# Where the first batch's zeros, masks and plain values are made: VectorE and GpSimd against ScalarE and SyncE

## Chip, cores and metric

One of the eight cores of a Trainium2 chip runs the kernel. The metric is the device time of one execution in microseconds (us); lower is better. A core has five engines with queues of their own: TensorE (PE; its weight loads are listed as PEld), VectorE (DVE), ScalarE (ACT), GpSimd (POOL) and SyncE (SP). The last two issue most of the DMAs here.

## The reference

Attention with a local mask, followed by a feed-forward network (FFN) with a squared ReLU:

```python
# q, k, v: (8 batches, 8 heads, 576 positions, 64), float32
scores = q @ k.T / 8
rel = pos[:, None] - pos[None, :]
mask_plain = (rel >= 0) & (rel < 32)                      # heads 0 to 3
mask_dil = (rel >= 0) & (rel < 128) & (rel % 4 == 0)      # heads 4 to 7
attn = softmax(where(mask, scores, -1e9))
x = (attn @ v) as (4608 tokens, 512)
h = maximum(x @ w_in, 0)          # w_in: (512, 2048)
out = (h * h) @ w_out             # w_out: (2048, 512)
```

## The kernel before

Everything is computed in bf16 with f32 accumulation. Heads are taken in pairs e = 0 to 3; pairs 0 and 1 are the plain ones, 2 and 3 the dilated ones. A batch's 576 positions fall into nine blocks of 64. A pair's values lie block-diagonally in a tile `vbd[b % 2]` of 128 x (4 pairs, 9 blocks, 128): the first head in rows and columns 0 to 63, the second in 64 to 127, and the other two quarters must be zero. Keys of later batches lie in `kbd` in the same way. Positions are split in two parts, 0 (256 positions) and 1 (320).

The FFN's tokens are cut into tiles, 256 tokens each for the first four, then 512. Each tile gives groups of matmuls: first layer (line 667, output `pf`, then a ReLU on ScalarE, line 678, and a square on VectorE, line 679), then second layer (line 699, then a copy to `osb`, line 705, and a store by SyncE). `kts` is the order in which the four slices of x (one for each pair) are summed up, and `early` says that a tile's first units are computed in two halves. The list `groups[:NF]` (line 804) orders the groups of the first two tiles.

All engines' work is put in order by hand. The string `PROGRAM` is cut by bars: what stands before the first bar is emitted first, what stands between two bars after the FFN group of that number. Its codes:

- `L0:q001` loads q and k of batch 0, part 0, pairs 0 and 1, on GpSimd's queue with a cast to bf16 (line 161); `v0d` loads the dilated values of part 0 (line 184), `v0p` the plain ones as four small DMAs straight into `vbd` (line 178), `v1dr` and `v1p` those of part 1, where `r` is the dilated pairs' last block (line 197); `i0` to `i3` load the four column slices of w_in (line 753), `o0` to `o3` those of w_out (line 758); `z` and `y` are zeroings by GpSimd for batch 1.
- `w21` and `W5` are so many idle matmuls (`turn`, line 465) on a zeroed tile `idle`, of 256 and 128 columns.
- For batch 0, with pair e and part: `T` transposes q and k on TensorE (line 495), `C` copies the result to SBUF (lines 502 to 510; `a` by ScalarE, `v` by VectorE), `B` adds the mask as a bias by matmul (line 536), `S` the scores (line 555), `E` their exponential on ScalarE (line 560), `P` the product with the values (line 586), `D` the sums (line 602), `L` and `X` the reciprocal of these as exp(-ln) on ScalarE (lines 609, 612), `M` the product that gives x in `xT` (line 619).
- `1q1`, `1k1` and so on are the same kind of steps of later batches.

Before the string is run, line 713 loads the mask patterns, VectorE zeroes `idle`, the quarters of `vbd[0]` and `kbd` (lines 716 to 727), and ScalarE makes masks for later batches by copies (`put`, line 731).

Of the kernel before, what the change touches and what calls it, by code (L numbers as in the profile page):

```python
# [12 lines left out]
RES = 4  # L13
# [5 lines left out]


PROGRAM = (
# [42 lines left out]
def kernel(  # L64
# [9 lines left out]
    nc = tc.nc  # L74
# [11 lines left out]
    NE = H // 2  # L86
# [366 lines left out]
            pv(b, e, part)  # L453

    first = {}
    sides = [slice(64 * hl, 64 * hl + 64) for hl in range(2)]

    def turn(n: int, cols: int):


        if "W" not in first:
            pool, nm = (ps_f, "pf") if ("P", 2, 0) in first else (ps_o, "po")
            first["W"] = pool.tile([P, 512], f32, name=nm)
        for _ in range(n):
            nc.tensor.matmul(
                first["W"][:, 0:cols], idle[:, 0:P], idle[:, 0:cols], start=True, stop=True, skip_group_check=True
            )

    def first_step(code: str):
# [88 lines left out]
        elif what == "E":  # L558
            ps = first.pop(("S", e, part))
            nc.scalar.activation(pts[e][:, c : c + ps.shape[1]], ps, ACT.Exp, scale=SCALE)  # L560
        elif what == "P":
            if ("P", *pair) not in first:
                if pair in ((2, 0), (2, 1), (0, 1)):
                    od = ps_o.tile([P, 512], f32, name="po"), ps_d.tile([P, 512], f32, name="pd")
                else:
                    od = [ps_a.tile([P, 512], f32, name="pa") for _ in range(2)]
                first.pop("W", None)
                first["P", *pair] = od
            o, d = [x[:, y0 : y0 + w] for x in first["P", *pair]]
            o3, d3 = byr(o), byr(d)  # L570
            pt = pts[e]
            bl = blocks(0, e, part)
            y, dms = c, []
            for x, (i, r, q0, q1) in enumerate(bl):
                z = (q1 - q0) * (RES if r is None else 1)
                quads = dil and i < 8
                for rows in sides if quads else [slice(0, P)]:
                    if r is None:
                        to, rhs = o3[rows, :, q0 - m0 : q1 - m0], byr(pt[rows, y : y + z])
                    else:  # L580
                        to, rhs = o3[rows, r, q0 - m0 : q1 - m0], pt[rows, y : y + z]
                    if quads:
                        lhs = vds[0][rows, e - NE // 2, i // RES, D * (i % RES) : D * (i % RES) + D]
                    else:
                        lhs = vbd[0][:, e, i, :]
                    nc.tensor.matmul(
                        to, lhs, rhs, start=(x == 0 and y0 == 0), stop=(x == len(bl) - 1), skip_group_check=True
                    )
                if not dil:
                    dms.append((d3[:, :, q0 - m0 : q1 - m0], byr(pt[:, y : y + z])))  # L590
                y += z
            if dil and part == 0:
                dms.append((d, pt[:, 0:w]))
            elif dil:
                main = byr(pt[:, c : c + 448])
                dms += [(d3, main[:, :, 32:112]), (d3[:, :, 0:32], main[:, :, 0:32]),
                        (d3[:, :, 64:80], byr(pt[:, c + 448 : c + 512]))]
            first["D", e, part] = dms
        elif what == "D":
            dms = first.pop(("D", e, part))  # L600
            for x, (dd, rh) in enumerate(dms):
                nc.tensor.matmul(
                    dd, ones, rh, start=(x == 0 and y0 == 0), stop=(x == len(dms) - 1), skip_group_check=True
                )
        else:
            n = 512 if part == 0 else w
            if what == "L":
                first["X", e, part] = rec = r_pool.tile([P, 512], f32, name="rec")
                nc.scalar.activation(rec[:, 0:n], first["P", e, part][1][:, 0:n], ACT.Ln)
            elif what == "X":  # L610
                rec = first["X", e, part][:, 0:n]
                nc.scalar.activation(rec, rec, ACT.Exp, scale=-1.0)
            else:
                o, rec = first["P", e, part][0][:, 0:n], first.pop(("X", e, part))[:, 0:n]
                to = xT[:, e, RES * m0 : RES * m0 + n]
                if part == 0:
                    to = xT[:, e : e + 2, 0:w]
                    o, rec = [x.rearrange("p (e n) -> p e n", e=2) for x in (o, rec)]
                nc.vector.tensor_tensor(out=to, in0=o, in1=rec, op=ALU.mult)
# [24 lines left out]
    def ffn_groups(tk0: int, nt: int):  # L644

        early = 0 < tk0 <= 2 * NT
        h2 = h2_pool.tile([P, NF, NT], bf16, name="h2T")
        per = NT // nt  # L650
        kts = (0, 2, 1, 3) if tk0 >= NT else (2, 3, 0, 1)
        cut = 3 if tk0 >= NT else 2
        cur, acc = {}, {}

# [24 lines left out]
            nc.vector.tensor_tensor(out=hv, in0=hv, in1=hv, op=ALU.mult)  # L679

        def g1(i):
            if i < 2 and early:
                for u in (2 * i, 2 * i + 1):
                    mm1(u, kts[:cut])
            elif i < 4 and early:
                for u in (2 * i - 4, 2 * i - 3):
                    mm1(u, kts[cut:])
            else:
                mm1(i, kts)
# [25 lines left out]
    def zero_halves(t):  # L715
        nc.vector.memset(t[0:64, :, :, 64:128], 0.0)
        nc.vector.memset(t[64:128, :, :, 0:64], 0.0)

    def zero_values(t, es, blocks):
        nc.vector.memset(t[0:64, es, blocks, 64:128], 0.0)  # L720
        nc.vector.memset(t[64:128, es, blocks, 0:64], 0.0)

    nc.vector.memset(idle[:, :], 0.0)
    zero_values(vbd[0], slice(0, NE // 2), slice(0, NB))
    zero_values(vbd[0], slice(NE // 2, NE), slice(8, NB))
    zero_halves(kbd)
    zero_values(vbd[0], slice(NE // 2, NE), slice(0, 8))
    near = mk[:, 0:96].rearrange("p (r m) -> p r m", r=RES)

    def put(dst, src):  # L730
        nc.scalar.copy(dst, src)

    def r4(ap):
        return ap.rearrange("p (r m) -> p r m", r=RES)

    put(mask_p[:, 0:288].rearrange("p (i c) -> p i c", c=96), mk[:, 0:96].unsqueeze(1).broadcast_to([P, 3, 96]))
    put(r4(mask_p[:, 288:352]), near[:, :, 0:16])
    put(r4(mask_p[:, 352:384]), near[:, :, 16:24])
    put(mask_p[:, 384:768].rearrange("p (i c) -> p i c", c=96), mk[:, 0:96].unsqueeze(1).broadcast_to([P, 4, 96]))
    put(r4(mask_p[:, 768:832]), near[:, :, 0:16])  # L740
    mh = mask_h[:, 0:352].rearrange("p (r c) -> p r c", r=2)
    put(mh[:, :, 0:96], mk[:, 160:256].unsqueeze(1).broadcast_to([P, 2, 96]))
    put(mh[:, :, 96:176], mk[:, 160:240].unsqueeze(1).broadcast_to([P, 2, 80]))
    put(mask_h[:, 352:416], mk[:, 96:160])
    put(r4(mask_d[:, 0:256]), mk[:, 160:224].unsqueeze(1).broadcast_to([P, RES, 64]))
    md = r4(mask_d[:, 256:704])
    put(md[:, :, 0:32], mk[:, 224:256].unsqueeze(1).broadcast_to([P, RES, 32]))
    put(md[:, :, 32:112], mk[:, 160:240].unsqueeze(1).broadcast_to([P, RES, 80]))
    put(mask_d[:, 704:768], mk[:, 96:160])

    def load_w_in(x):

# [15 lines left out]
    def run(code):  # L768
# [4 lines left out]
        elif code == "z":  # L773
            nc.gpsimd.memset(vbd[1][0:64, :, :, 64:128], 0.0)
            nc.gpsimd.memset(vbd[1][64:128, :, :, 0:64], 0.0)
        elif code[0] in "wW":
            turn(int(code[1:]), 256 if code[0] == "w" else P)
        elif code[0] in "TCBSEPDXM" or code[0] == "L" and code[2:3] != ":":
            first_step(code)
        elif code[0] != "L":  # L780
# [20 lines left out]
        groups += ffn_groups(tk0, nt)  # L801

    head = groups[:G]
    groups[:NF] = [head[y] for y in (0, 1, 2, 3, 16, 17, 18, 19, 4, 5, 20, 21, 6, 7, 22, 23)]
    groups[NF:G] = [head[y] for y in (8, 9, 12, 13, 10, 11, 14, 15)] + head[24:32]
    for b in range(5, B):
        at = {"a": (-2, 8), "b": (0, 8), "o": (3, 8), "p": (6, 8), "v": (-4, 8)}
# [51 lines left out]
```

## Time and profile before

| | us |
|---|---|
| median of 10 runs | 313.56 (312.99 to 314.64) |
| profiled execution | 315.54 |
| its span, first to last instruction | 313.6 |
| busy in the span: PE / DVE / ACT / POOL | 301.9 / 195.7 / 194.2 / 96.2 |
| mean granted TensorE clock | 0.995 of full |
| first matmul of the FFN's first layer starts | 18.66 |
| last stretch of the head's first layer (79 matmuls) | 27.71 to 36.50 |
| second layer's first matmul starts | 36.33 |

The span is read from the first instruction on; the profiled execution's own time also holds what lies around the span. Matmul ends are modelled, so one stretch can end after the next begins. DMA speeds are of bytes at the destination, which are half of those read where a load casts f32 to bf16.

### The profile page before, as it was taken

The page shows a single profiled execution, that of the slowest core. Times are in us where ns is not written, and L with a number is a line of the kernel's source. Part 1 is how long each engine was busy: PE and PEld are TensorE (multiplying, and loading weights), DVE is VectorE, ACT ScalarE, POOL GpSimd, SP SyncE. Part 2 cuts the span into 40 slices and gives each one's busy share as a digit, 9 for nine tenths or more (in the row PEclk, how much of TensorE's full clock was granted, in tenths as well). Part 3 has the DMA queues.
Part 4 walks back from the last instruction along what each step waited for, and adds up shares of the span by engine and source line. Part 5 has one row for each costly group of instructions (what it writes and reads, how often), then busy time and mean ns, then how long its engine had stood idle before and what let it go on. Part 6 is the DMA issues. An engine that isn't in the chain of part 4 may idle for free.

```text
span 313.6 us, 6784 instructions
## 1 busy us (share of the span) xinstructions
PE 301.9 (96%) x2553; PEld 189.4 (60%) x2585; DVE 195.7 (62%) x635; ACT 194.2 (62%) x416; POOL 96.2 (31%) x142
## 2 busy tenths in 40 slices
PE   7899999999998999999999999999999999999995
PEld 5689845968754555555589655555555555445543
DVE  6435348898977988984799469946995334104400
ACT  6377537859968955786478646864686456216511
POOL 8689865646308326601451041000000000000000
PEclk9989999999999999999999999999999999999999
DMA  7999999999999969999699985702200210121022
GB/s 106 132 158 200 210 170 173 177 126 195 163 133 149 169 132 187 164 118 186 91 143 119 136 141 93 131 3 67 69 0 0 70 68 2 33 67 33 2 67 67
DMA packets 79808, 34.91 MB, mean 111 GB/s; under 512 B 49824, under 2 KB 74784, under 8 KB 79776
## 3 DMA queue, kind: packets, MB, share of 16 engines
q0 software_dynamic: 47680, 18.36, 53.7%
q1 hardware_dynamic: 31952, 15.93, 28.6%
q8 instruction: 20, 0.33, 0.4%
q10 hardware_dynamic: 144, 0.20, 0.2%
q14 instruction: 12, 0.10, 0.1%
HBM read 36.90 MB, written 9.44 MB: 148 GB/s over the span
## 4 chain that ended last, share of the span: by engine, by line
PE 79%; DMA 6%; ACT 5%; DVE 4%; issue 2%; POOL 2%; ACTq 0%; POOLq 0%
PE pf L667 36%; PE pf L699 34%; PE po L413 3%; DMA vd<-in_v_dram 2%; PE pd L415 2%; DMA w_in<-in_moe_w_in_dram 2%; PE pa L304 2%; ACT h2T L678 1%; PE pa L310 1%; DMA out_dram<-osb 1%; ACT qT L248 1%; ACT rec L417 1%; ACT rec L418 1%; DVE xT L428 1%; POOL qb L161 1%
## 5 line engine op out<-in xcount | busy, mean ns | idle before, releaser
L667 PE MATMUL pf<-xT,w_in 128*128 128x256 bf16 (+1 forms) x758 | 132.7, 325 | 1.9 <-DMA w_in<-in_moe_w_in_dram 0.4
L699 PE MATMUL pf<-w_out_sb,h2T 128*128 128x512 bf16 (+1 forms) x570 | 130.9, 373 | 1.7 <-ACT osb L705 0.5
L667 PEld LDWEIGHTS <-w_in 128*128 128x128 bf16 x768 | 82.3, 113 | 37.1 <-issue 1.9
L678 ACT ACTIVATE h2T<-pf 128x512 bf16<-128x512 f32 x144 | 83.8, 598 | 25.0 <-PE pf L667 24.2
L699 PEld LDWEIGHTS <-h2T 128*128 128x128 bf16 x592 | 54.3, 98 | 53.9 <-issue 0.7
L679 DVE TENSOR_TENSOR h2T<-h2T 128x512 bf16<-128x512 bf16 x144 | 58.0, 422 | 41.1 <-ACT h2T L678 39.4
L705 ACT COPY osb<-pf 128x512 f32<-128x512 f32 (+1 forms) x37 | 21.2, 572 | 45.0 <-PE pf L699 44.9
L428 DVE TENSOR_TENSOR xT<-po,rec 128x288 bf16<-128x288 f32 (+2 forms) x52 | 23.7, 456 | 31.1 <-ACT rec L418 30.6
L178 POOL DMA_DIRECT2D vbd<-in_v_dram x40 | 28.2, 728 | 42.4 <-PE pd L415 38.7
L417 ACT ACTIVATE rec<-pd 128x288 f32<-128x288 f32 (+2 forms) x52 | 21.5, 413 | 24.1 <-PE pd L415 23.9
L314 ACT ACTIVATE pt<-pa 128x352 bf16<-128x352 f32 (+6 forms) x56 | 27.6, 499 | 8.6 <-PE pa L310 4.7
L418 ACT ACTIVATE rec<-rec 128x288 f32<-128x288 f32 (+2 forms) x56 | 24.9, 444 | 1.8
L413 PEld LDWEIGHTS <-vbd 128*128 128x128 bf16 x286 | 16.8, 97 | 10.4 <-DVE vbd L207 1.0
L248 DVE COPY qT<-xx 64x288 bf16<-64x288 bf16 x80 | 19.7, 246 | 1.1
L191 POOL DMA_DIRECT2D vd<-in_v_dram x24 | 14.6, 623 | 17.0 <-DMA kb<-in_k_dram 8.5
L252 DVE COPY kbd<-xx 64x288 bf16<-64x288 bf16 x40 | 18.8, 470 | 1.5 <-DMA xx<-kb 0.9
L161 POOL DMA_DIRECT2D qb<-in_q_dram x18 | 12.9, 718 | 20.2 <-DMA xx<-qb 16.3
L413 PE MATMUL po<-pt,vbd 128*128 128x96 bf16 (+3 forms) x263 | 18.0, 199 | 0.6 <-DVE xT L428 0.2
L415 PE MATMUL pd<-pt,mk 128*128 128x96 bf16 (+5 forms) x158 | 16.4, 204 | 0.0
L161 POOL DMA_DIRECT2D kb<-in_k_dram x18 | 12.8, 710 | 1.9 <-PE pf L415 1.1
L304 PE MATMUL pa<-qT,kbd 128*128 128x96 bf16 (+2 forms) x146 | 12.2, 201 | 1.0 <-ACT qT L248 1.0
L197 POOL DMA_DIRECT2D vbd<-in_v_dram x16 | 9.6, 604 | 10.9 <-PE pd L415 5.1
(81 smaller groups left out, 234.6 us busy)
## 6 DMA issues: line engine op xcount, KB each, us to landing
out_dram<-osb SPq DMA_DIRECT2D x18, 128.0 KB, 3.2
qb<-in_q_dram POOLq DMA_DIRECT2D x7, 320.0 KB, 8.3
kb<-in_k_dram POOLq DMA_DIRECT2D x7, 320.0 KB, 9.0
vd<-in_v_dram POOLq DMA_DIRECT2D x32, 64.0 KB, 6.6
w_in<-in_moe_w_in_dram POOLq DMA_DIRECT2D x4, 512.0 KB, 7.1
w_out_sb<-in_moe_w_out_dram POOLq DMA_DIRECT2D x4, 512.0 KB, 13.0
qb<-in_q_dram POOLq DMA_DIRECT2D x7, 256.0 KB, 7.2
kb<-in_k_dram POOLq DMA_DIRECT2D x7, 256.0 KB, 8.8
```

The costliest lines, as they stand in the source:

```text
L161: nc.gpsimd.dma_start(t[0:n, part, hs, :], src[b, hs, t0 : t0 + RES * n, :].rearrange("h (p r) d -> p h (r d)", r=RES))
L178: nc.gpsimd.dma_start(dst[rows, e, i0:i1, rows], v[b, 2 * e + hl, 64 * i0 : 64 * i1, :].rearrange("(i p) d -> p i d", p=64),)
L248: copy(qT[rows, e, :, m0 : m0 + n].rearrange("p (c j) m -> p j c m", j=2)[:, jj, :, :], src)
L314: nc.scalar.activation(pt[:, off : off + n], ps[:, 0:n], ACT.Exp, scale=SCALE)
L413: nc.tensor.matmul(oo, vb[:, e, i, :], rh, start=(x == 0), stop=(x == len(mms) - 1), skip_group_check=True)
L417: nc.scalar.activation(rec[:, 0:n], d[:, 0:n], ACT.Ln)
L418: nc.scalar.activation(rec[:, 0:n], rec[:, 0:n], ACT.Exp, scale=-1.0)
L428: nc.vector.tensor_tensor(out=tok, in0=o if o is o3 else o[:, 0:n], in1=rec if o is o3 else rec[:, 0:n], op=ALU.mult)
L667: nc.tensor.matmul(acc[u][:, nt * x + y0 : nt * x + y1], w_in_sb[piece][:, kt, c0 : c0 + 509 : 4], xT[:, kt, t0 : t0 + y1 - y0], start=(kt ...
L678: nc.scalar.activation(hv, acc[u][:, :].rearrange("p (x n) -> p x n", x=per), ACT.Relu)
L679: nc.vector.tensor_tensor(out=hv, in0=hv, in1=hv, op=ALU.mult)
L699: nc.tensor.matmul(cur[m][:, c0:c1], h2[:, f, P * m : P * m + P], w_out_sb[:, f, c0:c1], start=(f == 0), stop=(f == NF - 1),)
```

## The change

ScalarE zeroes the quarters of `vbd[0]` that batch 0 needs, by copies from `idle`. The zeros of `kbd`, those of the dilated pairs' first eight blocks and the mask copies move behind FFN group 16, the first of the second layer (codes `m`, `n`). Idle matmuls take 512 (`w`) and 256 (`W`) columns. Batch 0's plain values are no longer loaded by GpSimd: `g0` and `g1` load them with SyncE as f32 into three `osb` buffers, behind a tiny memset by VectorE, and `h0` and `h1` cast them into `vbd` by VectorE. The order of batch 0's steps and of the first FFN groups is new, the first and second tile are split differently into halves, and the plain pairs' part 0 uses `pf` buffers for its output and sums.

```diff
-    "L0:q001 L0:q023 L0:q101 L0:q123 L0:v0d L0:v0p L0:i0 L0:v1dr L0:i1 L0:v1p L0:i2 L0:i3 L0:o0 L0:o1 L0:o2 "
-    "L0:o3 L1:q00123 z y L1:v0dp L1:q10123 L1:v1dpr w21 T00 C00a T10 C10a B00 B10 S00 E00 B20 S10 E10 B30 T20q "
-    "B01 W5 T20k C20v T30 C30v B11 W2 S20 E20 W3 S30 E30 T01 C01v T11 C11v W2 S01 E01 T21 C21v B21 S11 E11 T31 "
-    "C31v P20 P30 D20 D30 L20 X20 M20 P00 P10 D00 D10 L00 X00 M00 B31 S21 E21 S31 E31 W4 | | P21 P31 D21 D31 "
-    "L21 X21 M21 L31 X31 M31 | | P01 P11 D01 D11 L01 X01 M01 L11 X11 M11 | | | | | | | | | | | | | | | | | | "
+    "L0:q001 L0:q023 L0:v0d L0:q101 L0:q123 L0:i0 L0:v1d L0:i1 L0:i2 L0:i3 L0:o0 L0:o1 L0:o2 L0:o3 L1:q00123 z "
+    "y L1:v0dp L1:q10123 L1:v1dpr w9 T00 C00a g0 T10 C10a B00 B10 S00 E00 B20 S10 E10 B30 W2 T20q T20k C20v "
+    "T30 C30v h0 W3 S20 E20 W1 S30 E30 P00 P10 D00 D10 L00 X00 T01 C01v g1 M00 T11 C11v B01 B11 P20 P30 D20 "
+    "D30 L20 X20 M20 S01 T21 C21a T31 C31v E01 S11 E11 | B21 S21 E21 h1 | B31 S31 E31 P21 P31 D21 D31 L21 X21 "
+    "M21 L31 X31 M31 P01 P11 D01 D11 L01 X01 M01 L11 X11 M11 | | | | | | | | | | | | | | | m n | | | | | "
...
+    def load_plain(part: int):
+        if part == 0:
+            plain[0] = t = osb_pool.tile([P, DM], f32, name="osb")
+            nc.vector.memset(t[:, 0:512:256], 0.0)
+            to = [t[:, 256 * e : 256 * e + 256] for e in range(2)]
+        else:
+            plain[1] = ts = [osb_pool.tile([P, DM], f32, name="osb") for _ in range(2)]
+            for t in ts:
+                nc.vector.memset(t[:, 0:448:64], 0.0)
+            to = [t[:, 0:320] for t in ts]
+            for hl, rows in enumerate(sides):
+                nc.sync.dma_start(
+                    ts[0][rows, 320:448].rearrange("p (h d) -> p h d", d=D),
+                    v[0, H // 2 + hl : H : 2, 512:S, :].rearrange("h p d -> p h d"),
+                )
+        for e in range(2):
+            for hl, rows in enumerate(sides):
+                nc.sync.dma_start(
+                    to[e][rows, :].rearrange("p (i d) -> p i d", d=D),
+                    v[0, 2 * e + hl, 256 * part : 256 + 320 * part, :].rearrange("(i p) d -> p i d", p=64),
+                )
+
+    def cast_plain(part: int):
+        for rows in sides:
+            if part == 0:
+                x = plain[0][rows, :].rearrange("p (e i d) -> p e i d", e=2, d=D)
+                nc.vector.tensor_copy(vbd[0][rows, 0:2, 0:4, rows], x)
+            else:
+                x = plain[1][0][rows, 320:448].rearrange("p (e d) -> p e d", d=D)
+                nc.vector.tensor_copy(vbd[0][rows, 2:4, 8, rows], x)
+                for e in range(2):
+                    x = plain[1][e][rows, 0:320].rearrange("p (i d) -> p i d", d=D)
+                    nc.vector.tensor_copy(vbd[0][rows, e, 4:NB, rows], x)
...
+        rhs = idle[:, :].unsqueeze(1).broadcast_to([P, cols // 256, 256])
         for _ in range(n):
             nc.tensor.matmul(
-                first["W"][:, 0:cols], idle[:, 0:P], idle[:, 0:cols], start=True, stop=True, skip_group_check=True
+                to[:, 0:cols], idle[:, 0:P], rhs, start=not at, stop=not at, skip_group_check=True
...
-                    od = [ps_a.tile([P, 512], f32, name="pa") for _ in range(2)]
+                    pool, nm = (ps_a, "pa") if part else (ps_f, "pf")
+                    od = [pool.tile([P, 512], f32, name=nm) for _ in range(2)]
...
-        early = 0 < tk0 <= 2 * NT
+        early = NT <= tk0 <= 2 * NT
...
-        kts = (0, 2, 1, 3) if tk0 >= NT else (2, 3, 0, 1)
+        kts = (0, 2, 1, 3) if tk0 >= NT else (0, 1, 2, 3) if tk0 == 0 else (2, 3, 0, 1)
...
-            if i < 2 and early:
+            if i < 2 and tk0 < NT:
+                for u in range(2):
+                    mm1(u, kts[2 * i : 2 * i + 2])
+            elif i < 2 and early:
...
-    zero_values(vbd[0], slice(0, NE // 2), slice(0, NB))
-    zero_values(vbd[0], slice(NE // 2, NE), slice(8, NB))
-    zero_halves(kbd)
-    zero_values(vbd[0], slice(NE // 2, NE), slice(0, 8))
+    for es, bs in ((slice(0, NE // 2), slice(0, NB)), (slice(NE // 2, NE), slice(8, NB))):
+        for hl in range(2):
+            to = vbd[0][64 * hl : 64 * hl + 64, es, bs, 64 - 64 * hl : 128 - 64 * hl]
+            none = idle[64 * hl : 64 * hl + 64, 0:64].unsqueeze(1).unsqueeze(1).broadcast_to(list(to.shape))
+            nc.scalar.copy(to, none)
...
+        elif code == "m":
+            masks()
...
+        elif code == "n":
+            zero_halves(kbd)
+            zero_halves(vbd[0][:, NE // 2 :, 0:8, :])
...
-    groups[:NF] = [head[y] for y in (0, 1, 2, 3, 16, 17, 18, 19, 4, 5, 20, 21, 6, 7, 22, 23)]
+    groups[:NF] = [head[y] for y in (0, 1, 16, 2, 3, 17, 18, 19, 4, 5, 20, 21, 6, 7, 22, 23)]
```

`masks` holds the old mask copies, word for word.

More of the change, by code (lines that the diff above doesn't have):

```diff
@@ L455 @@
     first = {}
-    sides = [slice(64 * hl, 64 * hl + 64) for hl in range(2)]
[L458 to L463, printed above, removed]
+    plain = {}
+    def load_plain(part: int):
[19 more added lines that the diff above has]
+                )
@@ L464, in turn @@
+    sides = [slice(64 * hl, 64 * hl + 64) for hl in range(2)]
+    def turn(n: int, cols: int, at=None):
+        if at:
+            to = first["S", at[0], at[1]]
+        else:
+            to = first["W"] = first.get("W") or ps_o.tile([P, 512], f32, name="po")
+        rhs = idle[:, :].unsqueeze(1).broadcast_to([P, cols // 256, 256])
         for _ in range(n):
             nc.tensor.matmul(
-                first["W"][:, 0:cols], idle[:, 0:P], idle[:, 0:cols], start=True, stop=True, skip_group_check=True
+                to[:, 0:cols], idle[:, 0:P], rhs, start=not at, stop=not at, skip_group_check=True
@@ L717, in zero_halves @@
         nc.vector.memset(t[64:128, :, :, 0:64], 0.0)
-    def zero_values(t, es, blocks):
-        nc.vector.memset(t[0:64, es, blocks, 64:128], 0.0)
-        nc.vector.memset(t[64:128, es, blocks, 0:64], 0.0)
     nc.vector.memset(idle[:, :], 0.0)
-    zero_values(vbd[0], slice(0, NE // 2), slice(0, NB))
-    zero_values(vbd[0], slice(NE // 2, NE), slice(8, NB))
-    zero_halves(kbd)
-    zero_values(vbd[0], slice(NE // 2, NE), slice(0, 8))
+    for es, bs in ((slice(0, NE // 2), slice(0, NB)), (slice(NE // 2, NE), slice(8, NB))):
[3 more added lines that the diff above has]
+            nc.scalar.copy(to, none)
     near = mk[:, 0:96].rearrange("p (r m) -> p r m", r=RES)
@@ L734, in r4, with masks @@
         return ap.rearrange("p (r m) -> p r m", r=RES)
[L736 to L749, printed above, removed]
+    def masks():
+        put(mask_p[:, 0:288].rearrange("p (i c) -> p i c", c=96), mk[:, 0:96].unsqueeze(1).broadcast_to([P, 3, 96]))
+        put(r4(mask_p[:, 288:352]), near[:, :, 0:16])
+        put(r4(mask_p[:, 352:384]), near[:, :, 16:24])
+        put(mask_p[:, 384:768].rearrange("p (i c) -> p i c", c=96), mk[:, 0:96].unsqueeze(1).broadcast_to([P, 4, 96]))
+        put(r4(mask_p[:, 768:832]), near[:, :, 0:16])
+        mh = mask_h[:, 0:352].rearrange("p (r c) -> p r c", r=2)
+        put(mh[:, :, 0:96], mk[:, 160:256].unsqueeze(1).broadcast_to([P, 2, 96]))
+        put(mh[:, :, 96:176], mk[:, 160:240].unsqueeze(1).broadcast_to([P, 2, 80]))
+        put(mask_h[:, 352:416], mk[:, 96:160])
+        put(r4(mask_d[:, 0:256]), mk[:, 160:224].unsqueeze(1).broadcast_to([P, RES, 64]))
+        md = r4(mask_d[:, 256:704])
+        put(md[:, :, 0:32], mk[:, 224:256].unsqueeze(1).broadcast_to([P, RES, 32]))
+        put(md[:, :, 32:112], mk[:, 160:240].unsqueeze(1).broadcast_to([P, RES, 80]))
+        put(mask_d[:, 704:768], mk[:, 96:160])
     def load_w_in(x):
@@ L775, in run @@
             nc.gpsimd.memset(vbd[1][64:128, :, :, 0:64], 0.0)
+        elif code == "m":
+            masks()
+        elif code[0] == "g":
+            load_plain(int(code[1]))
+        elif code[0] == "h":
+            cast_plain(int(code[1]))
+        elif code == "n":
+            zero_halves(kbd)
+            zero_halves(vbd[0][:, NE // 2 :, 0:8, :])
         elif code[0] in "wW":
-            turn(int(code[1:]), 256 if code[0] == "w" else P)
+            n, _, at = code[1:].partition("+")
+            turn(int(n), 512 if code[0] == "w" else 256, [int(x) for x in at])
         elif code[0] in "TCBSEPDXM" or code[0] == "L" and code[2:3] != ":":
```

## The prediction, made before the change was run

> **What bounds the kernel now.** I read the page first, for the share of each engine, then the chain of waits in order of time, then the timelines of TensorE (PE) and GpSimd (POOL) over the first 45 us, and last a table of clock and DMA by 5 us stretches.
>
> ```profile
> PE   7899999999998999999999999999999999999995
> PE 79%; DMA 6%; ACT 5%; DVE 4%; issue 2%; POOL 2%; ACTq 0%; POOLq 0%
> ```
> TensorE is busy 96% of the span and makes 79% of the chain that ends last. From about 28 us on there is almost nothing to win. The DMA's 6% lies at the front, and the chain shows where:
>
> ```profile
> 5.77 0.56 POOL kb L161
> 6.33 7.74 DMA vd<-in_v_dram
> 14.07 0.28 issue
> 14.36 0.59 POOL vd L184
> 14.95 1.16 POOL vbd L197 x2
> 16.10 6.57 DMA w_in<-in_moe_w_in_dram
> 22.71 1.94 PE pf L667 x16
> 25.36 0.45 ACT rec L609
> 26.21 0.43 ACT rec L609
> 27.17 0.50 DVE xT L619
> 27.71 8.79 PE pf L667 x79
> ```
> GpSimd issues loads, is held up behind a load of values, and so issues the second slice of w_in only at 16.10; it lands at 22.67. Two FFN groups (16 matmuls) wait for it, the last softmax of batch 0 follows them, and from 27.71 the first FFN layer runs without a stop: 79 matmuls in 8.79 us, 0.111 us each. GpSimd's timeline shows the hold:
>
> ```profile
> 8.11 0.62 POOL L178 DMA_DIRECT2D vbd<-in_v_dram x1 [0.53 <-DMA qb<-in_q_dram]
> 9.22 0.61 POOL L178 DMA_DIRECT2D vbd<-in_v_dram x1 [0.48 <-DMA kb<-in_k_dram]
> 12.35 0.75 POOL L753 DMA_DIRECT2D w_in<-in_moe_w_in_dram x1 [0.49 <-DMA qb<-in_q_dram]
> ```
> With each load's time to landing added to its issue, the eleventh load waits for the third, the twelfth for the fourth, the first w_in (the fifteenth) for the seventh: eight may be under way. So four small loads of plain values (L178) hold w_in back from about 8 us to 12.35, and the DMA engines run dry meanwhile (31 GB/s from 13.00 to 14.00). Last, the clock:
>
> ```profile
> 10.00:15.00 5.00, 4.30 (x124) 3.25 (x126) 2.27 (x8) 1.91 (x4) 3.21 (x6) 0.98 1.11 113
> 15.00:20.00 5.00, 4.95 (x84) 4.25 (x80) 1.80 (x4) 3.40 (x7) 4.59 (x8) 0.68 1.24 186
> ```
> The last three columns are granted clock, DMA share and GB/s. In finer cuts the clock is 0.50 from about 14.8 to 18.1.
>
> **What the Trainium skill says.** "TensorE: Matmul & The Clock Gate", Part 1: the array starts at half clock and is released, or cut again, after a window of about 3.4 us. The trace agrees in length (14.8 to 18.1), though the window before it was not idle: PE shows 4.30 busy of 5.00. "DMA: Bandwidth & Descriptors", section SWDGE vs HWDGE vs iDMA: a cast needs GpSimd's path, and DMAs of all issuers interleave on the same 16 engines. So SyncE can load the values only as f32, with a later cast, and its loads take DMA time from the others. The first is seen in the casts of the diff, the second in no row of this stage. For the price of a cast: "VectorE: DVE Perf Modes", the errata table, 58 + elements/2 cycles at 0.96 GHz if a double rate applies.
>
> **The change part by part.**
>
> *Zeros.* VectorE loses eight memsets, 1.07 to 6.48 us in its timeline. They delay the key copies of the first two transposes (L510), which start at 6.52 although the transposes ended near 5.6; the first scores wait for them until 7.00 (0.76 idle). Now the first key copy can start near 5.5 and the scores near 6.0 to 6.2: 0.8 us earlier locally. It helps little further on, since the next q and k land at 7.8 and 8.9 (issue 2.60 plus 5.2, 3.2 plus 5.7). ScalarE takes four copies: mask rows give 0.212 us for 32 and 0.505 for 384 elements, so 0.83 ns each; 1152 elements cost 1.14, 128 cost 0.29, together 2.9 us from the end of the table load (2.03) to 4.9. The twelve mask copies that stood at 3.20 to 6.08 are gone from there, so ScalarE is free before the first q copy at 5.5. Cover: ScalarE had nothing else; were it 1 us slower, 0.4 us would show.
>
> *Masks and remaining zeros, moved.* Mask copies 1.25+0.72+1.10 = 3.1 us on ScalarE, memsets 2x1.02+2x0.48 = 3.0 us on VectorE, now behind the first group of the second FFN layer. ScalarE idles there 4.58 us (until 41.71), VectorE 5.28 (until 42.87), so nothing shows. Without that cover up to 3 us of batch 1's copies would slip.
>
> *Idle matmuls.* 9x512 columns replace 21x256 (4608 for 5376). The early ones took 0.22 us per 256, so 9 wide ones end near 4.8, before the transposes at 5.13: cost 0. Later, 12 of 128 columns plus 4 at the end become 6 of 256; they stand in waits. What they do to the clock the trace can't tell: between -1.7 us (the cut of 3.4 us at half rate is avoided) and +1.7 (it comes in the FFN instead). I take -0.3, since I expect the cut to fall where PE waits for w_in anyway.
>
> *GpSimd's queue.* Ten issues leave it (4 + 4 plain, 2 of the 512-to-575 rest), at about 0.65 us: 6.5 us of issuing; two vd loads move before batch 0's second q/k part. The first w_in becomes the eleventh load, held only by the third (7.8), so is issued at 8.3 instead of 12.35. It queues behind q, k and vd on the DMA engines. Ahead of it and its own are 192 KB of masks, 1152 of q and k, 128 of vd and 512 of w_in, 2.03 MB, plus 0.26 MB of f32 values. By 9.5 us 1.07 MB had moved (GB/s summed over the stretches); the rest at 0.195 MB/us, the rate from 10 to 12 us, takes 6.3: 15.8, and landing some 0.4 later, 16.2 (before: 12.35+5.5 = 17.85). The second slice follows with 0.65 MB more, near 19.5 against 22.67. Thus the wait at 22.71 goes. w_out follows earlier too, so the second layer at 36.33 finds it.
>
> *Plain values on SyncE.* A tiny memset puts each batch of loads behind a VectorE copy: the first four go out near 6.0. A SyncE issue took 0.568 us (median, stores), so the last leaves at 7.7. Landing after issue: 2.4 us (the mask load, engines nearly free) to 5.8 (stores among loads). With 2.8 I get 10.5. Its bounds give 10.1 to 13.5. SyncE has nothing else to do until the first store at 42.32, so nothing waits behind its waits. Then two casts (h0), each 64x512: 0.33 us by the page's price, 0.59 without the double rate; I take 0.4.
>
> *The new order.* P00 stands right behind S30 on PE, so all of PE's queue, T01 onward, stands behind the casts. Call the landing A. One cast later P00 starts (A+0.45); P00 P10 D00 D10 take 1.2 (before 1.57 at half clock); T01 ends at A+1.9; two VectorE copies (0.33+0.48) and the memset of g1 at A+3.0. SyncE then issues six loads, 3.0 us at 0.5, and the fifth lands at about A+8.5; two casts, 0.6. Behind these casts (h1) on VectorE stand the squares of the first FFN units and M21, which are due later anyway. P21 and P31 with D21 and D31 take 1.5, and L21 to M31 follow as in the rows at L609 to L619: 0.44+0.47+0.42+0.47+0.49 = 2.3, of which 0.5 ran beside. So group 16 of the head starts at about A+12.4. There 8+104 = 112 of the 128 matmuls remain (16 stood ahead, from w_in's landing at 16.2), 112x0.111 = 12.4. The layer ends at A+24.8: for A = 10.5, 35.3 us. Before it ended at 36.4. With the clock's -0.3 partly inside this sum I keep 35.4: a gain of 1.0 us.
>
> *FFN groups.* The first tile's matmuls are split in halves so that the first 8 need M00 alone: M00 is due at A+3.7 = 14.2, before w_in at 16.2. Their number doesn't change.
>
> The sum: profiled span 313.6 (315.54 with what lies around it) becomes 312.6 (314.5). The median of the runs is 313.56, 0.04 below the span; less 1.0 it gives 312.5.
>
> **The rivals.**
> *Full gain.* Values land near 9.5 and the clock isn't cut at all: A+24.8 = 34.3, 2.1 us less: 311.4. For it: DMA engines were dry for a while before; against: SyncE's issue alone ends at 7.7.
> *No gain that lasts.* The chain of plain values takes the exact place of the w_in wait: A near 11.5, end 36.3: 313.5. For it: before, w_out landed (issue 24 plus 16.0) at 40.0, just ahead of its use, so the layers behind were matched to the old pace.
> *Slower: plain values land late and block PE's order.* The mechanism is P00 behind h0 behind SyncE's loads, and again P21 behind h1. Price: 1 us per us beyond A = 11.6, at which point it decides. At A = 12.8, or with g1's loads taking 1.3 us longer, it ends at 37.6: 314.8. For it: stores on SyncE's queue took 5.8 us and 128-byte value loads on the old queue 5.2 to 6.1 each; against: the new ones don't wait behind w_in in one ring. That the zeros' move does nothing by itself is inside the second case.
>
> **How the numbers follow.** Forecast 0.42 (312.5, own range 312.0 to 313.0); full gain 0.16; no gain 0.19; slower 0.23. The bound of 0.2% is 0.63 us, so 312.93 and 314.19, about what a measurement can tell from no change. Faster: 0.39 of the forecast's chance and all of the full gain's, 0.55; within: 0.03+0.19 = 0.22; slower: 0.23. The range leaves out the better half of the full gain and the worse half of the slower case: 311.3 to 314.8.
>
> **What would show it.** Right: no memset on VectorE before 5 us but one; key copies at 5.5; w_in's first slice issued near 8.3 and used near 16; PE's wait for w_in at 22.71 gone; the first layer's end near 35.4. Wrong: PE idle before P00 beyond 11.6, or before P21 beyond 20; a clock of 0.50 inside the long FFN stretch; mask copies or memsets that push batch 1's first copies past 42.9; w_in landing after 17.9.

## The result, and the profile after

The changed kernel took 336.95 us (median of 9 runs) against 313.60 for the kernel before (31 runs): a ratio of 1.0737, interval 1.0720 to 1.0753, or 23.4 us more. The profiled execution took 336.47 us, its span 334.7.

The page of the changed kernel, slices of TensorE's busy time and the shares of the chain of waits:

```profile
PE   8164189999999999999999999999999999999995
PE 80%; DMA 7%; ACT 5%; DVE 3%; issue 2%; SPq 1%; ACTq 0%; DVEq 0%
```

TensorE now has holes among the first six slices (8.4 us each) and is as busy as before after that. So the loss lies within the first 50 us. The chain of waits of the changed kernel there, with start, length and what:

```profile
8.24 1.12 SPq L476
9.40 9.43 DMA osb<-in_v_dram
18.92 0.43 DVE vbd L486
19.40 0.77 PE pf L627 x8
...
22.25 0.59 SPq L470
...
24.92 14.97 DMA osb<-in_v_dram
39.98 0.48 DVE vbd L492
...
45.53 12.94 PE pf L708 x112
58.73 5.78 PE pf L743 x26
```

Before, the same chain ran through GpSimd's loads of values and w_in; w_in is gone from it. In its place stand two loads of plain values that SyncE issues: 9.43 and 14.97 us. The second layer starts at 58.30 instead of 36.33, 22.0 us later. TensorE's timeline puts two waits to that, each behind a cast on VectorE:

```profile
19.40 0.77 PE L627 MATMUL pf<-pt,vbd 128*128 128x96 bf16 x8 [9.61 <-DVE vbd L486]
40.77 0.23 PE L627 MATMUL po<-pt,vbd 128*128 128x64 bf16 x1 [12.06 <-DVE vbd L489]
```

Together they are 21.7 us. VectorE waited in turn, as its own timeline says, for the loads:

```profile
17.87 0.42 DVE L486 CAST vbd<-osb 64x512 bf16<-64x512 f32 x1 [8.67 <-DMA osb<-in_v_dram]
37.17 0.48 DVE L492 CAST vbd<-osb 64x320 bf16<-64x320 f32 x1 [6.50 <-DMA osb<-in_v_dram]
39.98 0.48 DVE L492 CAST vbd<-osb 64x320 bf16<-64x320 f32 x1 [2.33 <-DMA osb<-in_v_dram]
```

The cast that TensorE's second wait names (line 489, at 40.49) had its own load long before, at 32.7. It stood behind the cast at 39.98 in VectorE's order, and that one waited for the fifth of the six loads.

The view of DMA issues gives each load's time from issue to landing. The four loads of `g0` (issued 6.76 to 10.3) took 6.5, 8.5, 9.5 and 9.4 us; of the six of `g1` (22.25 to 27.6) the two small ones took 8.0 and 9.9, the other four 13.6 to 15.7. GpSimd's timeline for the same time shows what else was queued:

```profile
7.51 0.84 POOL L795 DMA_DIRECT2D w_in<-in_moe_w_in_dram  x1
8.26 1.28 POOL L184 DMA_DIRECT2D vd<-in_v_dram  x2
9.42 0.89 POOL L795 DMA_DIRECT2D w_in<-in_moe_w_in_dram  x1
10.47 0.75 POOL L795 DMA_DIRECT2D w_in<-in_moe_w_in_dram  x1 [0.16 <-issue]
12.64 0.74 POOL L795 DMA_DIRECT2D w_in<-in_moe_w_in_dram  x1 [1.42 <-DMA kb<-in_k_dram]
13.74 0.54 POOL L800 DMA_DIRECT2D w_out_sb<-in_moe_w_out_dram  x1 [0.36 <-DMA qb<-in_q_dram]
```

The weights are issued 4.8 to 9.5 us earlier than before (12.35, 16.10, 20.00, 20.77, 21.50 for the first five). The first two land little earlier: the first slice at 17.6 (before 17.8), the second at 21.2 (22.7); the third and fourth land about 4 us earlier. They stand in the queue, in front of or beside the plain values.

### The profile page after: what moved, and what is told of

Its sections match the earlier page's. It is cut to its first block, busy times and chain, and to the rows that moved or that the text cites. A ratio compares the mean times of both kernels' runs of the same rounds, so it can differ in the third digit from the quotient of the medians.

```text
span 334.7 us, 6760 instructions
## 1 busy us (share of the span) xinstructions
PE 303.2 (91%) x2531; PEld 188.8 (56%) x2563; DVE 197.1 (59%) x641; ACT 197.7 (59%) x421; POOL 90.0 (27%) x132
## 4 chain that ended last, share of the span: by engine, by line
PE 80%; DMA 7%; ACT 5%; DVE 3%; issue 2%; SPq 1%; ACTq 0%; DVEq 0%
PE pf L708 34%; PE pf L743 34%; DMA osb<-in_v_dram 7%; PE po L413 3%; PE pd L415 2%; PE pa L304 2%; PE po L505 1%; PE pa L310 1%; ACT h2T L719 1%; SPq L476 1%; ACT qT L248 1%; PE pa L235 1%; DVE kbd L252 1%; ACT rec L417 1%; DVE xT L428 1%
## 5 line engine op out<-in xcount | busy, mean ns | idle before, releaser
L720 DVE TENSOR_TENSOR h2T<-h2T 128x512 bf16<-128x512 bf16 x144 | 57.8, 422 | 39.9 <-ACT h2T L719 38.5
L749 ACT COPY osb<-pf 128x512 f32<-128x512 f32 (+1 forms) x37 | 21.2, 572 | 42.2 <-PE pf L743 40.0
L178 POOL DMA_DIRECT2D vbd<-in_v_dram x32 | 23.0, 739 | 77.5 <-PE pd L415 57.1
L314 ACT ACTIVATE pt<-pa 128x352 bf16<-128x352 f32 (+6 forms) x56 | 27.6, 499 | 8.5 <-PE pa L310 4.7
L413 PEld LDWEIGHTS <-vbd 128*128 128x128 bf16 x286 | 16.9, 97 | 10.1 <-issue 0.7
L252 DVE COPY kbd<-xx 64x288 bf16<-64x288 bf16 x40 | 18.8, 470 | 0.6
L627 PEld LDWEIGHTS <-vbd 128*128 128x128 bf16 x22 | 1.7, 131 | 23.2 <-DVE vbd L489 12.2
L627 PE MATMUL po<-pt,vbd 128*128 128x96 bf16 (+2 forms) x7 | 0.8, 251 | 13.2 <-DVE vbd L489 12.1
```

The costliest lines, as they stand in the source:

```text
L178: nc.gpsimd.dma_start(dst[rows, e, i0:i1, rows], v[b, 2 * e + hl, 64 * i0 : 64 * i1, :].rearrange("(i p) d -> p i d", p=64),)
L314: nc.scalar.activation(pt[:, off : off + n], ps[:, 0:n], ACT.Exp, scale=SCALE)
L413: nc.tensor.matmul(oo, vb[:, e, i, :], rh, start=(x == 0), stop=(x == len(mms) - 1), skip_group_check=True)
```

## The experiments

Theories at this point: **A**, the queues take turns row by row on the DMA engines, so small rows lose against large ones; **B**, f32 rows of 256 bytes from SyncE are slow by themselves; **C**, a SyncE load waits in step with how much GpSimd has queued. And a rival to all three: the zeros, the idle matmuls or the new order of steps cost part of it.

### Parts of the change alone

**zeros_alone**: the kernel before, zeros and masks moved.

```diff
-    zero_values(vbd[0], slice(0, NE // 2), slice(0, NB))
...
+            nc.scalar.copy(to, none)
...
-... X01 M01 L11 X11 M11 | | | | | | | | | | | | | | | | | | "
+... X01 M01 L11 X11 M11 | | | | | | | | | | | | | m n | | | | | "
```

> The kernel before with the zeros, masks and key zeros moved as in the change, and nothing else. Main theory (the slowdown comes from SyncE's value loads alone; early zeros only bring the first scores forward, which then wait for the next q and k): first scores start 0.5 to 1.0 us earlier, time within 0.6 us of before (313 to 314). Rival (moving the zeros itself costs, through ScalarE or the clock): 315 or more, with a longer half-clock stretch.

313.79 us (22 runs) against 313.68 (40): ratio 0.9996, interval 0.9980 to 1.0013. The first scores start at 6.48 instead of 7.00, as TensorE's timeline shows:

```profile
6.48 0.34 PE L555 MATMUL pf<-xx 64*64 64x96 bf16 x8 [0.26 <-DVE xx L510]
```

So the half microsecond is won and is worth nothing at the end. The profiled execution was one of the fastest of its kernel (312.64 us, span 310.7), the profiled one of the kernel before one of its slowest (315.54): the 2.9 us between these two spans are no effect, as the medians show.

**wide_idle**: the kernel before with the wider idle matmuls.

```diff
-    ... w21 T00 ... B01 W5 ... B11 W2 ... W3 ... C11v W2 ... E31 W4
+    ... w9 T00 ... B01 W3 ... B11 W1 ... W2 ... C11v W1 ... E31 W2
```

> The kernel before with idle matmuls of 512 and 256 columns in its own places (9 of 512; 3, 1, 2, 1 and 2 of 256), nothing else. If they keep the clock from being cut near 14.8 us and that is worth its 1.7 us: 312 or less. If the cut is hidden by other waits, or isn't avoided: 313 to 314.5.

314.07 us against 314.00: ratio 1.0023, interval 0.9998 to 1.0049, so no gain. Seven of the 20 executions took 316.4 to 317.1 us, where none of the 23 of the kernel before, in the same session, took over 315.4; what sets these seven apart isn't known. In 9 executions the mean clock was 1.000, so there was no cut in those, and they took 310.9 to 312.2 us of span, with the kernel before at 311.1 to 313.5. Whether one cut shows in the time is better read from the kernel before: over the sessions of all these runs, its twelve executions with a mean clock of 0.993 to 0.995 have a median of 314.5 us, 61 others, at 0.998 or more, one of 313.7 (a single one of 318.09, over 1.5% above the fastest, is left out). So about 0.8 us goes with a cut; no run here tests it by itself.

**plain_back**: all of the change but the plain values, which GpSimd loads again in the old places of its queue.

```diff
-L0:q001 L0:q023 L0:v0d L0:q101 L0:q123 L0:i0 L0:v1d L0:i1 L0:i2 L0:i3 ... g0 ... h0 ... g1 ... h1
+L0:q001 L0:q023 L0:q101 L0:q123 L0:v0d L0:v0p L0:i0 L0:v1dr L0:i1 L0:v1p L0:i2 L0:i3 ...
```

> The changed kernel with the plain values loaded by GpSimd with a cast, in the old queue order, and without the casts on VectorE; all else as changed. Main theory: the 23 us go away, 312 to 315. Rival (the new order of steps, or the idle matmuls, cost a good part): 318 or more, with PE waits that aren't for values.

319.94 us, ratio 1.0183 (1.0138 to 1.0228). 17.0 us of the loss are gone, 6.3 remain. The time is the rival's, and the new order has a part in it, but TensorE's longest wait is still one for values:

```profile
13.33 0.75 PE L627 MATMUL pf<-pt,vbd 128*128 128x96 bf16 x8 [2.91 <-DMA vbd<-in_v_dram]
```

The new order puts P00 ahead of T01. With plain values that land at 13.2, TensorE stands still for 2.9 us with work behind; before, P00 came last and waited for nothing. TensorE then works at half clock from 13.3 to 21.8, 8.5 us, where the kernel before did so for 3.4. By an estimate (half of the difference) that costs another 2.5 us. The two make most of the 6.3; which single step of the new order matters wasn't tested.

### Where the loads' time comes from

**no_gate**: the ten loads issued at the start, without the tiny memsets.

```diff
-            nc.vector.memset(t[:, 0:512:256], 0.0)
...
-                nc.vector.memset(t[:, 0:448:64], 0.0)
...
-    "L0:q001 L0:q023 L0:v0d ... C00a g0 T10 ... C01v g1 M00
+    "g0 g1 L0:q001 L0:q023 L0:v0d ... C00a T10 ... C01v M00
```

> The changed kernel with SyncE's ten value loads issued at the start, without the tiny memsets ahead of them, so before any weights are in GpSimd's queue. Theory A (the rows of SyncE's loads take turns with GpSimd's large weight rows): all land before 14 us, the PE waits of 9.6 and 12.1 us go, 311 to 316; the first q and k land 1 to 3 us later. Theory B (rows of 256 bytes from SyncE are slow by themselves, whatever else is queued): the last loads still take over 12 us and total 20 to 25 us from the start, so P21 waits, 317 to 325. Theory C (a new load waits for all that GpSimd queued before it): as A.

316.32 us (315.48 to 319.08 in 17 runs), ratio 1.0098 (1.0072 to 1.0124). All ten loads land by 14.5 us, each 2.8 to 7.7 us after its issue, and both long waits are gone. B falls: the same rows from the same issuer take 38 to 64% of the time. 20.6 of 23.4 us hang on when the loads are issued. TensorE's remaining waits in this kernel, with their line, cause, sum, number and longest:

```profile
PE po L624 <- DVE xT L657: 1.3, 1, 1.3
PE pa L532 <- DMA kb<-in_k_dram: 0.8, 2, 0.4
PE pf L705 <- DMA w_in<-in_moe_w_in_dram: 0.7, 1, 0.7
```

**wide_rows**: as changed, with one run of 1024 or 1280 bytes in place of four or five of 256.

```diff
-                    to[e][rows, :].rearrange("p (i d) -> p i d", d=D),
-                    v[0, 2 * e + hl, ...].rearrange("(i p) d -> p i d", p=64),
+                    to[e][rows, :],
+                    v[0, 2 * e + hl, ...].rearrange("(p i) d -> p (i d)", p=64),
```

> The changed kernel with one run of 1024 or 1280 bytes per partition in place of four or five runs of 256 bytes, same bytes, same places in SBUF: the plain pairs' values of a block are then other positions' values, so that part of the result differs. Theory A (turn by turn): landing shrinks with the number of rows, 9.4 to about 4 us and 15 to about 6 us, total 316 to 322. Theory B: likewise short. Theory C (behind the bytes that GpSimd has queued): no change, 9 and 15 us, total 333 to 337.

333.31 us, from one execution, as with the four kernels that follow. The last of the first four lands at 16.4 instead of 18.8; the fifth of the six, on which TensorE hangs, at 35.5, 12.7 us after its issue instead of 15.0. A fourth or fifth of the rows saves some 15 to 20% of the time, far from what was expected of A. But that expectation took each turn to be equally long, and it isn't. The queues' own counts show it (packets, MB, time as a share of 16 engines; a packet is one row, apart from a few of 4 bytes, q0 is GpSimd's queue, q1 SyncE's). First the changed kernel from 26 to 34 us, then from 34.5 to 38.5:

```profile
q0 software_dynamic: 433, 1.58, 97.3%
q1 hardware_dynamic: 422, 0.10, 9.6%
```

```profile
q0 software_dynamic: 898, 0.52, 88.6%
q1 hardware_dynamic: 901, 0.22, 42.5%
```

And wide_rows from 24 to 34 us:

```profile
q0 software_dynamic: 526, 1.89, 93.2%
q1 hardware_dynamic: 520, 0.32, 13.9%
```

Each time both queues move the same number of rows: one for one, as A has it. What a turn costs is set by GpSimd's row. In the first stretch its rows average 3.6 KB (w_out) and take 0.29 us of a DMA engine each, in the second 0.6 KB (the next q and k) and 0.06 us; both are worked out from the lines, as share times 16 engines times the stretch, over the packets. Nearly all the turns of wide_rows fell into the slow stretch, and about three quarters of those of the changed kernel into the fast one, after 34 us. So fewer rows saved little, and A stands. Turns aren't all of it: between issue at 22.25 and 26 us, no row of SyncE's moved at all.

**two_issuers**: the loads of pair 1, four of the ten, issued by ScalarE.

```diff
-                nc.sync.dma_start(
+                (nc.scalar if e else nc.sync).dma_start(
```

> The changed kernel with half of the plain loads (pair 1) issued by ScalarE in place of SyncE, so that they lie in two queues beside GpSimd's. Theory A (queues take turns): two queues get about twice the share, so landing falls from 9.4 and 15 us to about 6 and 9, time 325 to 331. Theory C (a load waits for what GpSimd queued before it): no change, 334 to 338.

335.19 us, 1.8 below the changed kernel's median. The view of DMA issues, over the time in which the six were issued:

```profile
osb<-in_v_dram ACTq DMA_DIRECT2D x2, 80.0 KB, 13.6
osb<-in_v_dram SPq DMA_DIRECT2D x2, 80.0 KB, 15.2
```

The queues from 25 to 34 us, where q10 is ScalarE's:

```profile
q0 software_dynamic: 472, 1.68, 92.6%
q1 hardware_dynamic: 470, 0.11, 9.5%
q10 hardware_dynamic: 466, 0.12, 6.0%
```

The Trainium skill ("DMA: Bandwidth & Descriptors", section Queues, rings and completion order) has each DMA engine serve its queues in turn. The trace agrees: three queues, three equal counts. So the second queue did bring twice the turns while GpSimd's long rows were moving. Little came of it. SyncE kept 896 of the 1536 rows of the six, its last load landed at 39.0 for 41.3, and the six had been issued 1.4 us earlier. TensorE's two waits fell to 5.0 and 8.3 us, but ScalarE's steps stood behind its own issuing, and TensorE worked 19.9 us at half clock instead of 8.6.

**weights_held**: GpSimd's weights held until the casts are done.

```diff
+        elif code[0] == "u":
+            nc.vector.memset(w_in_sb[int(code[1])][:, 0, 0:2], 0.0)
...
-h0 W3 ... E21 h1 |
+h0 u0 L0:i0 L0:v1d W3 ... E21 h1 u1 L0:i1 L0:i2 L0:i3 L0:o0 L0:o1 L0:o2 L0:o3 ... |
```

> The changed kernel with SyncE's loads where they were, but with GpSimd's queue held: the first slice of w_in and what follows it wait for the first casts (h0), the second slice and what follows it for the last casts (h1). Theory A/C (SyncE's loads are slow because large weight loads stand in GpSimd's queue): the first four loads land within 3 to 6 us of issue, PE's wait before P00 falls from 9.6 to under 4 us; the six later ones within 4 to 7 us, the wait of 12.1 us to under 3. The weights come late in turn, so the time is 320 to 330. Theory B (slow by themselves): landing stays 9 and 15 us, and with the late weights the time is over 340.

321.72 us. The first four land after 5.6 to 6.2 us; TensorE's wait before P00 is 5.7, more than expected. The six land after 3.2 to 4.1 us, and TensorE waits no longer before P21. The queues from 19 to 21 us, while the one weight load beside the six was moving (it landed at 21.2, two small loads by 22.0), and then from 21 to 24:

```profile
q0 software_dynamic: 503, 0.39, 127.1%
```

```profile
q1 hardware_dynamic: 1628, 0.39, 60.5%
q0 software_dynamic: 95, 0.04, 10.3%
```

In the first stretch q1 has no line: SyncE's rows had not begun. In the second they had the engines nearly to themselves. So this run shows the loads beside a queue that runs empty.

**gpsimd_f32**: the same f32 loads and casts in GpSimd's queue, ahead of the large weight loads.

```diff
-L0:q001 L0:q023 L0:v0d L0:q101 L0:q123 L0:i0 L0:v1d L0:i1
+L0:q001 L0:q023 g0 L0:v0d L0:q101 L0:q123 L0:i0 L0:v1d g1 L0:i1
...
-                nc.sync.dma_start(
+                nc.gpsimd.dma_start(
```

> The changed kernel with the same f32 loads and casts, but issued by GpSimd, the first four behind q and k of part 0, the six others behind the first slice of w_in. If a place far forward in the one queue is what counts: landing 5 to 8 us after issue, the first four by 12 us, 316 to 322. If the f32 rows of 256 bytes are the cost: landing over 9 us, 325 or more.

318.31 us; the first four land after 3.2 to 4.5 us, the six after 3.1 to 6.8. A place ahead of the weights does it, with issue from 3.8 us on instead of 6.8. But what is put behind waits: the next q is now 1.4 us late for TensorE.

**paced_weights**: as changed, but GpSimd has about two weight loads under way at a time.

```diff
+    def pace(piece):
+        if loaded:
+            n = len(loaded)
+            nc.gpsimd.tensor_copy(paced[:, n - 1 : n], loaded[-1])
+        loaded.append(piece)
```

> The changed kernel with GpSimd issuing a weight load only when the one before the last has landed (a copy of one column from it), so that about 1 MB is queued at a time in place of up to eight loads, while the DMA engines stay busy. If a SyncE load waits for the depth of GpSimd's queue (theory C): the first four land within 5 to 8 us, the six others within 5 to 9 us of issue, where they took 9 and 15, and the time is 318 to 328. If SyncE's queue just gets a small share of busy DMA engines: 9 and over 12 us, 330 to 340.

326.76 us. This was meant to part "busy engines" from "a deep queue". The stretch from 25 to 30 us, whose last columns are clock, DMA share and GB/s, and TensorE's two waits:

```profile
25.00:30.00 5.00, 4.44 (x74) 3.38 (x74) 0.99 (x4) 2.81 (x6) 0.72 (x2) 0.81 1.18 233
```

```profile
PE pf L627 <- DVE vbd L486: 8.2, 1, 8.2
PE po L627 <- DVE vbd L489: 1.7, 1, 1.7
```

The engines moved 233 GB/s, more than the changed kernel's 211 in the same stretch, and the six loads landed after 4.0 to 8.2 us instead of 8.0 to 15.7. TensorE's second wait fell from 12.1 to 1.7 us. That looks like C, a wait for the queue's depth and not for busy engines. The mean over 5 us hides what happened, though. The queues from 26 to 27 us, and then from 27 to 29:

```profile
q1 hardware_dynamic: 945, 0.23, 103.9%
q0 software_dynamic: 19, 0.06, 27.9%
```

```profile
q0 software_dynamic: 98, 0.40, 99.1%
q1 hardware_dynamic: 66, 0.02, 6.3%
```

With only about two weight loads under way, GpSimd's queue had hardly a row to move for 1 us, and in it SyncE moved more than half of its rows. As soon as w_out's rows were there, it fell back to some 33 a us. The depth of GpSimd's queue matters in so far as it keeps that queue from running empty. C as an order falls too: in the changed kernel the first of the six (issued at 22.25) landed at 30.25, before a w_out slice issued at 14.56, which landed at 31.5. The first wait fell only to 8.2: when those four were issued, pacing hadn't begun, and q, k, vd and two weight loads stood there already. Why SyncE's first row moves only some 4 us after its issue in the changed kernel stays open.

### What is left

**old_order**: the kernel before with its own order, zeros moved, and the ten f32 loads at the start.

```diff
-L0:q001 L0:q023 L0:q101 L0:q123 L0:v0d L0:v0p L0:i0 L0:v1dr L0:i1 L0:v1p L0:i2 L0:i3
+g0 g1 L0:q001 L0:q023 L0:q101 L0:q123 L0:v0d L0:i0 L0:v1d L0:i1 L0:i2 L0:i3
...
-C31v P20 ... X00 M00 B31
+C31v h0 P20 ... X00 M00 h1 B31
```

> The kernel before with its own order of steps and FFN groups and its idle matmuls, with the zeros moved, and with SyncE's ten f32 loads issued at the start, the casts behind C31v and M00. If the new order of steps is what leaves no_gate 2.7 us behind the kernel before: 311.5 to 314. If the f32 loads themselves (their share of the DMA engines, the later first q and k) are: 315 to 317.5.

319.34 us (316.51 to 319.96 in 6 runs), ratio 1.0157 (1.0120 to 1.0194): above no_gate, and outside both expectations. The new order is therefore not what holds no_gate back. How much better it is with early values is less clear. Both kernels' executions fall into two groups, 315.5 to 316.9 and 318.3 to 319.1 for no_gate, 316.5 to 316.6 and 319.3 to 320.0 here, so within a group the difference is about 0.7 us; the rest of the 3.0 between the medians is that 4 of 6 executions fell into the upper group here, and 7 of 17 there. TensorE's timeline shows one cost of the f32 loads here:

```profile
13.76 0.34 PE L530 MATMUL pa<-mk,kb 80*64 80x80 bf16 x8 [0.84 <-DMA kb<-in_k_dram]
```

k of part 1 lands at 13.7, and the first k at 6.1 where the kernel before needed it at 5.28. All executions of the two kernels with a mean clock of 0.979 or less are in the upper group, and one of no_gate's with 1.000 is there too. What makes an execution fall there wasn't pursued. No run here beats the kernel before.

## Why the prediction was wrong

Forecast 312.5, range 311.3 to 314.8, measured 336.95.

- **The step that failed** is "With 2.8 I get 10.5. Its bounds give 10.1 to 13.5", and, behind it, "the fifth lands at about A+8.5". A was 18.8, since the fourth load took 9.4 us, and the fifth of the six landed at 39.9, A+21.1. The upper bound of 5.8 us came from stores, issued at 42 us and later (and the first four of these took 4.7 to 7.2). A landing time was carried over from loads that had the engines nearly to themselves. The runs show what it depends on in its place: each of SyncE's rows took its turn with one row of GpSimd's queue (422 and 433 packets from 26 to 34 us, at 0.29 us a turn by the estimate above), and before that no row moved for 3.5 us after the first issue of `g0` and 3.7 after that of `g1`. The profile of before held a nearer row: GpSimd's own loads issued between 5.7 and 7 us took 6.9 to 7.7, and the w_out slices and the next q and k, issued into a full queue, 11.1 to 17.7. I used one of these numbers for another purpose and didn't ask whether a load on SyncE's queue would fare like them. weights_held and paced_weights show that it lands fast where GpSimd's queue runs empty.
- **The slower rival** had the waits and their place (TensorE's order behind `h0` and `h1`), and a chance of 0.23. It was mis-sized: A = 12.8 for 18.8, or 1.3 us more for the second batch where it was 12.6 more. The reason against it, "the new ones don't wait behind w_in in one ring", was true and no help, since the rings take turns. Its "5.2 to 6.1" for the small value loads is misread as well: those of part 0 took 3.8 to 6.4. That the same change which freed GpSimd's queue would fill it with weights sooner, and so delay the very loads it had moved away, was in neither: the values' bytes were added to w_in's sum, and nothing was set down for what w_in does to the values.
- **GpSimd's queue.** Issue of w_in at 8.3 was nearly right (7.51); its landing at 16.2 was not (17.6), nor the second slice's at 19.5 (21.2). The wait for w_in did vanish, because TensorE was later than w_in.
- **The new order's own sum** held between its waits: P00 at A+0.6 (said A+0.45), the memset of `g1` at A+3.3 (A+3.0), 112 matmuls in 12.4 us at full clock as in no_gate. SyncE's six issues took 5.4 us instead of 3.0.
- **Zeros** were right in kind: alone they brought scores 0.5 us earlier for the 0.8 said, and nothing at the end. In the changed kernel it was 0.2 us (6.77), as the scores waited for the memset of `g0`. **Masks and zeros moved** were hidden: ScalarE ran the mask copies from 58.99 on, behind the last ReLU.
- **Idle matmuls**: -0.3 us was said, wide_idle shows no gain. That a new cut of the clock would come with the waits was named as a bound of 1.7 us. It was more: the mean clock fell to 0.963. The cut stretches lie mostly in the waits themselves, but TensorE worked 8.6 us in them, against 3.4 in the kernel before, which by an estimate (half of the difference) cost 2.6 us. The cut stretches, first of the changed kernel, then of the kernel before, PE's busy time in the second column and the clock third from the end:

```profile
12.70:23.00 10.30, 3.60 (x62) 2.87 (x64) 2.32 (x8) 1.23 (x2) 5.11 (x8) 0.50 1.25 200
33.20:46.90 13.70, 5.00 (x56) 4.09 (x57) 4.30 (x10) 3.37 (x8) 8.07 (x14) 0.50 1.37 167
```

```profile
14.75:18.17 3.42, 3.42 (x67) 2.93 (x67) 1.31 (x3) 2.23 (x4) 3.42 (x6) 0.50 1.28 193
```

## What to carry to other kernels

A load that is moved to another queue "to get it out of the way" still shares the engines with the first queue, and freeing that queue lets it fill sooner with large transfers. Here the queues took turns row for row, so a load of many short rows is priced by its number of rows on an engine times the time of the other queue's row, not by its bytes, nor by the fastest landing in the trace. An average over some microseconds can hide this; count the packets of each queue in the stretch where the load moves. Where a step becomes the gate of an in-order engine, ask for the landing time at which it starts to cost, and leave that margin twice. And issue early what is small and needed early: here the same ten loads cost 23 us behind the weights and 3 in front of them.

## What the runs showed of the hardware that was not expected

- Queues with rows to move took turns, one row for one: 422 of SyncE's to 433 of GpSimd's, 901 to 898, and with ScalarE's as a third 470 to 472 to 466. The turn is as long as the other row: 0.29 us beside rows of 3.6 KB, 0.06 beside rows of 0.6 KB. So SyncE's 256-byte rows moved at some 53 a us (422 in 8 us) beside the former, 225 beside the latter (901 in 4), and 945 in a microsecond in which GpSimd's queue had 19.
- A cast of 64x512 from f32 in two times four blocks took 0.42 us, one of 64x128 in two blocks 0.22 (the other of the two 0.33), one of 64x320 in five blocks 0.48. 0.42 and 0.22 give 0.52 ns an element and 0.15 us fixed; the one of five blocks then took 1.03 ns an element, half the rate. The Trainium skill ("VectorE: DVE Perf Modes", Mode 2×_2P) asks for an outermost dimension that is even, or odd and equal in source and destination. Five is odd; which part of the condition failed here, no run shows. The prediction's 0.33 us for a 64x512 cast was too low, and its 0.4 near.
- A half-clock stretch of about 3.4 us in this stage (14.75 to 18.17 in the trace of before) came though TensorE had been busy for 2.73 of the 3.41 us ahead of it. Executions of the kernel before with a mean clock that fits one such cut are about 0.8 us longer than the others, as wide_idle's section says.
